# Attention and gated feed-forward on one core: another order of steps and copies for the first batch, output weights loaded in two parts

## The chip, the core and the metric

The kernel runs on one core of one Trainium2 chip. The metric is the device time of one execution in microseconds (us). Four runs of the kernel before the change took 518.34 to 519.17 us, with a median of 518.67 us. The profiled execution, which all rows come from, took 518.44 us; its span (first to last instruction) is 516.6 us.

The core has five engines with their own queues of instructions: TensorE (PE in the profile) multiplies matrices and writes into eight PSUM banks, ScalarE (ACT) and VectorE (DVE) copy and compute out of those banks, GpSimd (POOL) and SyncE (SP) issue the DMA transfers here. Each engine works through its queue in order.

## What is computed

```python
# q, k, v: (8 batches, 8 heads, 1024, 64);  E, F: (64, 1024)
k_proj = E @ k;  v_proj = F @ v                       # 64 projected keys and values per head
attn   = softmax(q @ k_proj.T / sqrt(64))
x      = (attn @ v_proj), heads side by side          # 8192 tokens x 512
gate   = sigmoid(x @ w_gate);  val = x @ w_val        # 512 -> 1536
out    = (gate * val) @ w_out                         # 1536 -> 512, float32
```

## The kernel before, in words

The work goes batch by batch; a batch is two blocks of 512 tokens. Attention for a batch gives `xT` (x with its 512 features on the partitions). The feed-forward part takes it block by block: `G` and `V` matmuls against `wG` and `wV`, a tanh on ACT in place of the sigmoid, a product on DVE into `hT`, and the output matmuls against `wO` (`oproj`, L1312). Later blocks build their products from seven half-size ones, with sums of weights and inputs made by DVE (`t_sums`, `vt_sums`, `xs_sums`, `product`).

The order in every queue is fixed when the kernel is built. `Plan.add` (L154) keeps one list of operations; each engine gets its own in that order, and a wait is set only where an operation reads or overwrites what another engine wrote. A PSUM bank counts as one object: every copy out of a bank waits for the copy before it if that was on another engine. From batch 1's second half on, a planner (`arranged`, L58) orders the list. Everything before that, which is all that the change edits, is an order written by hand: the sequence of calls at L1865 to L1905 for the first half of the first batch, and a list `todo` with additions by position (`put`, `on`) after it. The banks for the first half come from a written-out ring, `whole` (L358).

The first half of the first batch is worked out in two groups of four heads, R = 0 and R = 1:

- `start_loads` (L472) issues, on POOL's queue, k, q, k, q, v, v in halves by R (`load_kv_heads`, `load_q_half`), then the weights `wG` and `wV` in pieces. E and F come on SP's queue.
- `project_consts` (L604) turns E and F; `busy(n)` (L628) puts n filler matmuls of 128x512 into bank pF3 whose result nobody reads.
- `k_part(R)` (L1872) projects k (16 matmuls) and ACT copies the result to `kp` (`keep_k`, L660). `turn_k` (L684) transposes it and ACT copies to `kpD`. `qt(R)` (L715) transposes q into two banks, copied to `qT`.
- `sc(R)` (L738): scores, then two exponentials on ACT into `eT`. `den(R)` (L764): sums, and a reciprocal on DVE. `bc(R)` (L797): spreads the reciprocals over two banks; `keep(g)` (L818) copies bank g to `xu` on ACT.
- `v_part(R)` (L1877): projects v into two banks; `keep_v` (L670) makes four copies of a quarter each, on ACT, DVE, ACT, DVE, to `vpD`. `xo(R)` (L843): eight output matmuls into two banks, then DVE multiplies them with `xu` into `xT` (R = 0: two products of 128x512; R = 1: four of 128x256).
- `first_pair` (L1256) begins the feed-forward part: G for row groups 0 and 1 of `xT`, which R = 0 gives, then `xo(1)`, then V for the same row groups, then row groups 2 and 3.

`keep_v` has one more use, `v_alone` (L966), for batch 1 with all eight heads in one bank. `second_loads` (L1907) issues q, k and v of batch 1, four transposing DMAs of q on SP, and then one load of all `wO` on POOL's queue, which waits for the first two of these transposes. The loads of batch 2 come behind it in POOL's queue. The names `"wO"` and `"wO12"` in the lists of operands stand for `wO` and for the quarter of it that `t_sums(1)` overwrites.

Of the kernel before, what the change touches and what calls it, by code (L numbers as in the profile page):

```python
# [7 lines left out]
ALU = mybir.AluOpType  # L8
# [4 lines left out]
P = 128  # L13
# [224 lines left out]
def bass_linformer_attn__then__ffn_glu_sigmoid_kernel(  # L238
# [11 lines left out]
    B = q.shape[0]  # L250
# [6 lines left out]
    with contextlib.ExitStack() as es:  # L257
# [89 lines left out]
        class Ring:  # L347
# [9 lines left out]
        F0, F1, F2, F3 = FB  # L357
        whole = Ring(  # L358
            (A0, A1)
            + (A2, A3, F0, A0, A1, F1)  # L360
            + (A2, F2, A3, A0, F0)
            + (A2, A3, A1, F1, F2)
            + (A0, F0, A1, F1, A2, A3)
            + (A0, F3, A2, A3)
        )
        ffn, att = Ring(FB), Ring(AB)

# [289 lines left out]
                        tp=(0, 64 * h),  # L657
                    )

        def keep_k(bk, c0, R=None):  # L660
            width = 256 if R is None else 128
            act(
                kp[:, pairs(R), :],
                bank[bk][:, c0 : c0 + width],
                [],
                [("kp", x) for x in both(R)],
                b=bk,
            )

        def keep_v(bks, c0, engines, R=None):  # L670
            vv = vpD[:, :, :].rearrange("p (r h) d -> p r h d", h=2)
            width = 256 if R is None else 128
            for n, (h, g) in enumerate(((0, 0), (1, 1), (0, 1), (1, 0))):
                o = vv[64 * g : 64 * g + 64, pairs(R), h, :]
                i = bank[bks[h]][64 * h : 64 * h + 64, c0 : c0 + width].rearrange(
                    "p (r d) -> p r d", d=DH
                )
                ws = [("vpD", h, g, x) for x in both(R)]
                if engines[n] == "ACT":
                    act(o, i, [], ws, b=bks[h])  # L680
                else:
                    dve(lambda e, o=o, i=i: e.tensor_copy(o, i), [], ws, b=bks[h])  # L682

        def turn_k(ring, R=None):  # L684
            bk = ring.next()
            ob = bank[bk][:, :].bitcast(BF16)
            rs = range(NR)[pairs(R)]
            for n, r in enumerate(rs):
                for g in range(2):
                    mm(  # L690
                        bk,
                        ob[64 * g : 64 * g + 64, n * P : (n + 1) * P],
                        kp[:, r, :],
                        ident[:, :],
                        [("kp", r // 2), "ident"],
                        tr=True,
                        tp=(0, 64 * g),
                    )
            act(
                kpD[:, 2 * rs[0] : 2 * rs[-1] + 2, :].rearrange("p h c -> p (h c)"),  # L700
                ob[:, 0 : P * len(rs)],
                [],
                [("kpD", x) for x in both(R)],
                b=bk,
            )

        def VPD(R):
# [2 lines left out]
        def half_unit(hf, ring):  # L710
# [4 lines left out]
            def qt(R, engines):  # L715
                for rr, eng in enumerate(engines):
                    bk = ring.next()
                    ob = bank[bk][:, :].bitcast(BF16)
                    for x in range(2):
                        for t in range(2):  # L720
                            c = x * 2 + t
                            mm(
                                bk,
                                ob[:, c * P : (c + 1) * P],
                                Qb[:, 4 * R + 2 * rr + x, (2 * hf + t) * P : (2 * hf + t + 1) * P],
                                ident[:, :],
                                [("Q", hf, R), "ident"],
                                tr=True,
                            )
                    o = qv[:, R, 2 * rr : 2 * rr + 2, 256 * hf : 256 * hf + 256]  # L730
                    i = ob[:, 0:512].rearrange("p (x c) -> p x c", x=2)
                    ws = [("qT", hf, R, rr)]
                    if eng == "ACT":
                        act(o, i, [], ws, b=bk)
                    else:
                        dve(lambda e, o=o, i=i: e.tensor_copy(o, i), [], ws, b=bk)

            def sc(R):  # L738
                bks = [ring.next(), ring.next()]
# [57 lines left out]
            def bc(R):  # L797
                bks = [ring.next(), ring.next()]
                for c in range(4):
                    for g in range(2):  # L800
                        n = 2 * R + g
                        nn = slice(32 * n, 32 * n + 32)
                        mm(
                            bks[g],
                            bank[bks[g]][:, c * P : (c + 1) * P],
                            (bsel8 if hf else bsel8f)[nn, c, :, :].rearrange("p h d -> p (h d)"),
                            (rhl if hf else rden)[nn, 0:P],
                            ["bsel8", ("rhl", R)] if hf else ["bsel8f", ("rden", 0, R)],
                            tp=(32 * n, 0),
                        )  # L810
                def scales():
                    for g in range(2):
                        scale(R, g, bank[bks[g]], xu[:, 2 * R + g, :], [("xu", 2 * R + g)], bks[g])

                if hf:
                    return scales

                def keep(g):  # L818
                    act(
                        xu[:, 2 * R + g, :],  # L820
                        bank[bks[g]][:, :],
                        [],
                        [("xu", 2 * R + g)],
                        b=bks[g],
                    )

                return keep
# [15 lines left out]
            def xo(R):  # L843
# [14 lines left out]
                for g in range(2):  # L858
                    n = 2 * R + g
                    if hf:  # L860
                        act(xu[:, n, :], bank[bks[g]][:, :], [], [("xu", n)], b=bks[g])
                    elif R == 0:
                        scale(R, g, bank[bks[g]], xu[:, n, :], [("xu", n)], bks[g])
                if hf == 0 and R == 1:
                    for r in (2, 3):
                        for g in range(2):
                            cc = slice(256 * (r - 2), 256 * (r - 2) + 256)
                            dve(
                                lambda e, r=r, g=g, cc=cc: e.tensor_tensor(
                                    xT[s][:, r, hf, 256 * g : 256 * g + 256],  # L870
# [85 lines left out]
        def attention(b):  # L956
# [9 lines left out]
            def v_alone():  # L966
                bk = AA.take()
                turn_k(Ring((bk,)))
                AA.append(bk)
                bk = AA.take()  # L970
                project(1, 1, [bk, bk], 0)
                keep_v([bk, bk], 0, ["ACT", "DVE", "ACT", "DVE"])
                AA.append(bk)

            def sc_one(r, bks):
# [280 lines left out]
        def first_pair(blk, between):  # L1256
# [3 lines left out]
                for i in ii:  # L1260
                    mm_one(blk, m, i, n, pbs[m, n])

            step(0, "G", 0, 1)
            step(1, "G", 0, 1)
            if between:
                between()
            step(0, "V", 0, 1)
# [44 lines left out]
        def oproj(blk, tt, pb, cols=((0, DM),)):  # L1312
# [3 lines left out]
            for n, (c0, c1) in enumerate(cols):  # L1316
                if n:
                    pb = FF.take()
                for m in range(NF):
# [2 lines left out]
                        bank[pb][:, 0 : c1 - c0],  # L1322
                        hT[blk % 2][:, m, tt * P : (tt + 1) * P],
                        wO[:, m, c0:c1],
                        [("hT", blk % 2, m, tt // 2), "wO", "wO12"],
                        start=(m == 0),
                        stop=(m == NF - 1),
                    )
# [22 lines left out]
        def t_sums(n):  # L1351
# [1 line left out]
            B21, B22 = wO[:, H6:NF, 0:256], wO[:, H6:NF, 256:512]  # L1353
            T4, T3, T2 = [wT[:, i, :, :] for i in range(3)]
            o, a, b, op, r, w = {
                3: (T3, B22, B12, ALU.subtract, ["wO", "wO12"], [("wT", 3)]),
                2: (T2, T3, B11, ALU.add, ["wO", ("wT", 3)], [("wT", 2)]),
                4: (T4, B21, T2, ALU.subtract, ["wO", ("wT", 2)], [("wT", 4)]),
                1: (B12, B12, B11, ALU.subtract, ["wO"], ["wO12", ("wT", 1)]),
            }[n]  # L1360
            if n == 4:
                w = w + ["bsel8", ("kp", 0), ("kp", 1)]
# [28 lines left out]
        def product(blk, bk, A, B, start=False, stop=False, js=(0, 1), ms=(0, NF // 2), also=()):  # L1391
            h = hT[blk % 2]
            for j in js:
                for m in range(*ms):
# [8 lines left out]
                        rhs, k = wT[:, 4 - int(B[1]), m, :], ("wT", int(B[1]))  # L1403
                    else:
                        c = 256 * (B[2] == "2")
                        rhs, k = wO[:, m + H6 * (B[1] == "2"), c : c + 256], "wO"
                    mm(
                        bk,
                        bank[bk][:, 256 * j : 256 * j + 256],
# [456 lines left out]
        blocks_ready(0)  # L1866
        constants()
        project_consts()
        busy(5)
        qt, sc, den, bc, xo = half_unit(0, whole)  # L1870

        def k_part(R):  # L1872
            bk = whole.next()
            project(0, 0, [bk, bk], 0, R)
            keep_k(bk, 0, R)

        def v_part(R):  # L1877
            bks = [whole.next(), whole.next()]
            project(1, 1, bks, 0, R)
            keep_v(bks, 0, ["ACT", "DVE", "ACT", "DVE"], R)  # L1880

        k_part(0)
        qt(0, ("DVE", "DVE"))
        turn_k(whole, 0)
        busy(1)
        sc(0)
        busy(2)
        k_part(1)
        den(0)
        turn_k(whole, 1)  # L1890
        busy(1)
        qt(1, ("ACT", "DVE"))
        busy(1)
        sc(1)
        keep = bc(0)
        keep(0)
        keep(1)
        den(1)
        v_part(0)
        busy(1)  # L1900
        xo(0)
        keep = bc(1)
        keep(0)
        v_part(1)
        keep(1)  # L1905

        def second_loads():  # L1907
            load_q(1)
            load_k(1)
            load_v(1)  # L1910
            transpose_q()
            load(
                wO[:, :, :],
                moe_w_out.rearrange("(m p) c -> p m c", p=P),
                ["wO", "wO12"],
                "wO",
                r=turned()[:2],
            )


        todo, at = [], {}
# [200 lines left out]
```

## Time and profile before

| | |
|---|---|
| median of four runs | 518.67 us (518.34 to 519.17) |
| the profiled execution | 518.44 us, span 516.6 us |
| first FFN matmul to start | 21.19 us after the span's start |
| fillers in the first batch | 11 (5, 1, 2, 1, 1, 1) |
| landing of the k, q, k, q, v, v halves | 8.5, 9.8, 12.4, 13.7, 16.2, 18.8 us |
| load of `wO` | issued at 57.35 us, landed 12.2 us later; first matmul that reads it at 71.22 us |

Two rows of the page give the span in 40 slices of 12.9 us: the busy share of the DMA engines in tenths, and what they moved.

```profile
DMA  9999999899598778454946379374104330201013
GB/s 167 199 198 203 157 202 209 120 181 223 78 225 160 153 143 144 97 131 123 172 84 153 65 146 205 56 160 87 63 1 103 42 103 1 82 2 64 19 43 124
```

In a timeline row the first number is the start in us after the span's start, the second the time taken, then engine, line, operation, what is written <- what is read, shapes, and the count of merged instructions; in brackets the idle time of the engine before it and what ended it. Lines L385 (matmuls) and L389 (ACT) are helpers, so operations are told apart by their tiles: `KVs,EFT` is a projection, `gT,Qb` q being turned, `gT,wT` k being turned, `qT,kpD` scores, `eT,dsel` denominators, `gT,vT` the spread of reciprocals, `eT,vpD` outputs, and `gT` alone a filler. Some small tiles of the first batch lie inside buffers that later hold sums of weights, and the profile shows the buffer: `gT` is also `ident` and `rden`, `wT` also `kp`, `vT` also `bsel8f`.

### The profile page before, as it was taken

To read this page: it belongs to the slowest core of one execution; us is meant where nothing else is said; L and a number is where in the kernel's file an instruction comes from. 1 tells how busy PE (TensorE), PEld (TensorE's weight loads), DVE (VectorE), ACT (ScalarE), POOL (GpSimd) and SP (SyncE) were. 2 spreads that over 40 slices of the span, in tenths; PEclk is the share of its full clock that TensorE was granted. 3 is DMA by queue.
4 is the path that set the end of the run, shared out by engine and by line. 5 is a ranking of instruction groups with operands and counts; after the bars stand their busy time and mean duration, and the time that the engine had idled before them with its cause. 6 is when DMAs were issued, how large, how long until landed. Compare 5 with 4: busy or idle time off the path is not lost.

```text
span 516.6 us, 11359 instructions
## 1 busy us (share of the span) xinstructions
PE 505.0 (98%) x4595; PEld 410.4 (79%) x4595; DVE 409.9 (79%) x806; ACT 345.6 (67%) x646; POOL 40.4 (8%) x59
## 2 busy tenths in 40 slices
PE   5999999999999999999999999999999999999997
PEld 2545545888888888888888888888888888888885
DVE  4448789899779796987879888797968898787774
ACT  2555683867778677677767676777677766676752
POOL 9420201200200020000100020000000000000000
PEclk9999999999999999999999999999999999999999
DMA  9999999899598778454946379374104330201013
GB/s 167 199 198 203 157 202 209 120 181 223 78 225 160 153 143 144 97 131 123 172 84 153 65 146 205 56 160 87 63 1 103 42 103 1 82 2 64 19 43 124
DMA packets 105189, 63.13 MB, mean 122 GB/s; under 512 B 63024, under 2 KB 97328, under 8 KB 105136
## 3 DMA queue, kind: packets, MB, share of 16 engines
q0 software_dynamic: 33984, 29.89, 37.2%
q1 hardware_dynamic: 71152, 32.52, 27.4%
q8 instruction: 36, 0.59, 0.5%
q14 instruction: 17, 0.14, 0.1%
HBM read 60.29 MB, written 16.78 MB: 149 GB/s over the span
## 4 chain that ended last, share of the span: by engine, by line
PE 96%; DVE 1%; ACT 1%; DMA 1%; issue 0%; SPq 0%; DVEq 0%
PE pA L385 52%; PE pF L385 44%; DMA EF<-in_F_dram 1%; DVE hT L1830 0%; DVE vsnap L1708 0%; ACT vpD L389 0%; ACT vsnap L389 0%; DVE gT L780 0%; DVE vpD L682 0%; DVE ost L1435 0%; ACT sig L389 0%; DVE sig L1784 0%; ACT xu L389 0%; ACT qT L389 0%; ACT EF L389 0%
## 5 line engine op out<-in xcount | busy, mean ns | idle before, releaser
L389 ACT ACTIVATE sig<-pA 128x512 f32<-128x512 f32 x126 | 75.1, 596 | 45.9 <-PE pA L385 45.6
L1697 ACT ACTIVATE pF<-pA 128x512 f32<-128x512 f32 x99 | 58.5, 591 | 35.2 <-PE pA L385 30.1
L1708 DVE TENSOR_TENSOR vsnap<-pF,vsnap 128x512 f32<-128x512 f32 x90 | 61.7, 685 | 18.1 <-ACT vsnap L389 9.4
L1784 DVE TENSOR_TENSOR sig<-pF,sig 128x512 f32<-128x512 f32 x84 | 57.6, 685 | 4.4 <-PE pA L385 2.7
L385 PE MATMUL pF<-wO,hT 128*128 128x256 bf16 (+1 forms) x402 | 59.4, 285 | 0.0
L1830 DVE SCALAR_TENSOR_TENSOR hT<-sig,vsnap 128x512 bf16<-128x512 f32 x84 | 56.6, 684 | 1.0
L389 ACT ACTIVATE vsnap<-pA 128x512 f32<-128x512 f32 x84 | 50.2, 597 | 8.1 <-PE pA L385 7.8
L389 ACT ACTIVATE sig<-sig 128x512 f32<-128x512 f32 x84 | 52.7, 628 | 2.9 <-DVE sig L1784 2.5
L385 PE MATMUL pF<-xS,wV 128*128 128x256 bf16 x360 | 54.0, 273 | 0.1
L1830 DVE SCALAR_TENSOR_TENSOR hT<-sig,pF 128x512 bf16<-128x512 f32 x42 | 28.8, 685 | 30.7 <-PE pF L385 30.0
L385 PE MATMUL pA<-xT,gT 128*128 128x256 bf16 x336 | 50.5, 273 | 0.0
L385 PE MATMUL pA<-xT,vT 128*128 128x256 bf16 x336 | 50.4, 273 | 0.0
L385 PE MATMUL pF<-xS,wG 128*128 128x256 bf16 x336 | 50.4, 273 | 0.0
L385 PE MATMUL pF<-xT,wG 128*128 128x256 bf16 (+1 forms) x264 | 50.2, 311 | 0.0
L389 ACT ACTIVATE sig<-pF 128x512 f32<-128x512 f32 x66 | 39.5, 598 | 14.9 <-PE pF L385 12.5
L385 PE MATMUL pA<-wT,hT 128*128 128x256 bf16 x360 | 48.8, 273 | 0.5 <-ACT EF L389 0.4
L385 PEld LDWEIGHTS pF<-wO,hT 128*128 128x128 bf16 x402 | 38.7, 98 | 10.5 <-issue 0.8
L385 PE MATMUL pF<-xT,wV 128*128 128x256 bf16 (+1 forms) x240 | 41.5, 294 | 0.0
L385 PEld LDWEIGHTS pF<-xS,wV 128*128 128x128 bf16 x360 | 34.9, 98 | 6.1 <-DVE vsnap L1708 0.4
L385 PEld LDWEIGHTS pA<-wT,hT 128*128 128x128 bf16 x360 | 34.4, 98 | 6.0 <-ACT EF L389 1.4
L389 ACT ACTIVATE eT<-pA 128x512 bf16<-128x512 f32 x59 | 34.5, 594 | 5.4 <-PE pA L385 4.9
L385 PEld LDWEIGHTS pA<-xT,gT 128*128 128x128 bf16 x336 | 31.1, 98 | 7.5 <-issue 1.9
(158 smaller groups left out, 910.8 us busy)
## 6 DMA issues: line engine op xcount, KB each, us to landing
out_dram<-ost SPq DMA_DIRECT2D x61, 256.0 KB, 2.4
Qb<-in_q_dram POOLq DMA_DIRECT2D x7, 1024.0 KB, 10.8
KVs<-in_k_dram POOLq DMA_DIRECT2D x7, 1024.0 KB, 13.6
KVs<-in_v_dram POOLq DMA_DIRECT2D x7, 1024.0 KB, 17.8
wO<-in_moe_w_out_dram POOLq DMA_DIRECT2D x1, 1536.0 KB, 12.2
wG<-in_moe_w_gate_dram POOLq DMA_DIRECT2D x5, 256.0 KB, 17.1
wV<-in_moe_w_val_dram POOLq DMA_DIRECT2D x5, 256.0 KB, 17.7
KVs<-in_k_dram POOLq DMA_DIRECT2D x2, 512.0 KB, 8.2
```

The source lines that it names most:

```text
L385: return add("PE", lambda e: e.matmul(o, lhsT, rhs, **kw), r=r, x=[("bank", b)])
L389: return add("ACT", lambda e: e.activation(o, i, func, scale=scale), r=r, w=w, x=x, t=t)
L1697: lambda e: e.activation(bank[c][:, :], bank[a][:, :], AF.Copy, scale=1.0),
L1708: lambda e: e.tensor_tensor(o, bank[bk][:, :], o, ALU.add),
L1784: dve(lambda e: e.tensor_tensor(o, bank[bk][:, :], o, ALU.add), [key], [key], b=bk)
L1830: lambda e: e.scalar_tensor_tensor(o, sg.rearrange("p (j c) -> p j c", j=2), 1.0, x.rearrange("p (j c) -> p j c", j=2), ALU.add, ALU.mult,),
```

## The change

The written order of the first batch is another one, the ring of banks follows it, and copies go to other engines:

- Steps before: fillers 5, k0, q0, turn k0, filler, scores 0, fillers 2, k1, den 0, turn k1, filler, q1, filler, scores 1, bc 0, den 1, v0, filler, xo 0, bc 1, v1.
- Steps after: fillers 4, k0, fillers 2, q0, turn k0, filler, scores 0, filler, k1, fillers 2, turn k1, q1, den 0, fillers 2, scores 1, fillers 2, v0, den 1, bc 0, xo 0, bc 1, v1. That makes 14 fillers.
- Copies that go from ACT to DVE: k of group 1, both turned k, one of the two banks of bc 0. From DVE to ACT: one bank of q0 and the two DVE copies of v0. For q1 the two banks change engines. For v1 DVE makes the two copies of one bank and ACT those of the other, between ACT's two copies of bc 1, which change their order.
- `xo(0)` makes four products of 128x256, row group by row group, as `xo(1)` did; `xo(1)` now takes its second bank first. `first_pair` makes G row group by row group.
- `keep_v` takes the numbers of the copies and one engine. In `v_alone` ACT makes its two copies first, then DVE its two.
- `wO` is loaded in two halves by rows, each with its own name and semaphore (`wO0`, `wO1`), both behind the same wait; readers name the half that they read.

The core of the diff (banks of the ring, the helper `copied` that picks ACT or DVE, and the renamed operands left out):

```diff
-        def keep_v(bks, c0, engines, R=None):
+        def keep_v(bks, c0, ns, eng, R=None):
...
-            for n, (h, g) in enumerate(((0, 0), (1, 1), (0, 1), (1, 0))):
+            for n in ns:
+                h, g = ((0, 0), (1, 1), (0, 1), (1, 0))[n]
...
                     if hf:
                         act(xu[:, n, :], bank[bks[g]][:, :], [], [("xu", n)], b=bks[g])
-                    elif R == 0:
-                        scale(R, g, bank[bks[g]], xu[:, n, :], [("xu", n)], bks[g])
-                if hf == 0 and R == 1:
-                    for r in (2, 3):
-                        for g in range(2):
-                            cc = slice(256 * (r - 2), 256 * (r - 2) + 256)
+                if hf == 0:
+                    for r in (2 * R, 2 * R + 1):
+                        for g in (R, 1 - R):
+                            cc = slice(256 * (r - 2 * R), 256 * (r - 2 * R) + 256)
...
                 project(1, 1, [bk, bk], 0)
-                keep_v([bk, bk], 0, ["ACT", "DVE", "ACT", "DVE"])
+                keep_v([bk, bk], 0, (0, 2), "ACT")
+                keep_v([bk, bk], 0, (1, 3), "DVE")
...
-            step(0, "G", 0, 1)
-            step(1, "G", 0, 1)
+            step(0, "G", 0)
+            step(1, "G", 0)
+            step(0, "G", 1)
+            step(1, "G", 1)
...
-        busy(5)
+        busy(4)
...
-        k_part(0)
-        qt(0, ("DVE", "DVE"))
-        turn_k(whole, 0)
+        k_part(0, "ACT")
+        busy(2)
+        qt(0, ("DVE", "ACT"))
+        turn_k(whole, 0, "DVE")
         busy(1)
         sc(0)
+        busy(1)
+        k_part(1, "DVE")
         busy(2)
-        k_part(1)
+        turn_k(whole, 1, "DVE")
+        qt(1, ("DVE", "ACT"))
         den(0)
-        turn_k(whole, 1)
-        busy(1)
-        qt(1, ("ACT", "DVE"))
-        busy(1)
+        busy(2)
         sc(1)
+        busy(2)
+        v_part(0)(range(4), "ACT")
+        den(1)
         keep = bc(0)
-        keep(0)
-        keep(1)
-        den(1)
-        v_part(0)
-        busy(1)
+        keep(0, "ACT")
+        keep(1, "DVE")
         xo(0)
         keep = bc(1)
-        keep(0)
-        v_part(1)
-        keep(1)
+        keep(1, "ACT")
+        keep_1 = v_part(1)
+        keep_1((0, 2), "DVE")
+        keep_1((1, 3), "ACT")
+        keep(0, "ACT")
...
-            load(
-                wO[:, :, :],
-                moe_w_out.rearrange("(m p) c -> p m c", p=P),
-                ["wO", "wO12"],
-                "wO",
-                r=turned()[:2],
-            )
+            for x, w in enumerate((["wO0", "wO12"], ["wO1"])):
+                load(
+                    wO[:, H6 * x : H6 * x + H6, :],
+                    moe_w_out.rearrange("(m p) c -> p m c", p=P)[:, H6 * x : H6 * x + H6, :],
+                    w,
+                    f"wO{x}",
+                    r=turned()[:2],
+                )
```

## The prediction

> **What bounds it now.** I read the page first: busy shares, then the chain that ended last. TensorE is 98% busy, and the chain runs through matmuls almost all the way.
>
> ```profile
> PE 505.0 (98%) x4595; PEld 410.4 (79%) x4595; DVE 409.9 (79%) x806; ACT 345.6 (67%) x646; POOL 40.4 (8%) x59
> PE 96%; DVE 1%; ACT 1%; DMA 1%; issue 0%; SPq 0%; DVEq 0%
> ```
>
> So an edit pays only if it lets TensorE (PE) start its long run of feed-forward (FFN) matmuls earlier, or removes one of its few waits later. The PE timeline of the first 25 us shows the place. Columns: start, us taken, instruction, count, idle time before it and who ended it.
>
> ```profile
> 10.03 0.64 PE L385 MATMUL pA<-KVs,EFT 128*64 128x128 bf16 x16
> ...
> 15.51 0.41 PE L385 MATMUL pA<-qT,kpD 64*64 64x256 bf16 x8 [0.25 <-ACT qT L389]
> ...
> 18.07 0.39 PE L385 MATMUL pF<-gT 128*128 128x512 bf16 x1
> 19.19 0.30 PE L385 MATMUL pA<-eT,vpD 64*64 64x256 bf16 x2 [0.72 <-DVE vpD L682]
> ...
> 21.19 1.04 PE L385 MATMUL pF<-xT,wG 128*128 128x512 bf16 x4
> 22.18 0.84 PE L385 MATMUL pA<-eT,vpD 64*64 64x256 bf16 x8
> ```
>
> The reader is to see: the first FFN matmul starts at 21.19; before it PE stands 0.72 us for VectorE's (DVE's) copy of projected v. The chain of waits shows a second stop: the eight output matmuls that begin at 22.18 are cut in two, because their second bank is still being copied.
>
> ```profile
> 21.97 0.61 ACT xu L389
> 22.57 0.04 issue
> 22.62 0.41 PE pA L385 x6
> 23.02 0.97 PE pF L385 x4
> 23.99 0.03 issue
> 24.02 0.59 PE pF L385 x2
> ```
>
> From 24.02 PE hardly waits (the waits view has 0.9 us in three longer gaps up to the end). One of them, at 61.6, is touched by the change. The timeline of all engines there (pieces of other engines left out):
>
> ```profile
> 59.67 0.38 ACT L389 ACTIVATE vpD<-pA 64x256 bf16<-64x256 f32 x1 [0.16 <-PE pA L385]
> ...
> 60.08 0.43 DVE L682 CAST vpD<-pA 64x256 bf16<-64x256 f32 x1 [2.08 <-ACT vpD L389]
> ...
> 60.54 0.38 ACT L389 ACTIVATE vpD<-pA 64x256 bf16<-64x256 f32 x1 [0.49 <-DVE vpD L682]
> 60.94 0.60 ACT L389 ACTIVATE vsnap<-pF 128x512 f32<-128x512 f32 x1
> ...
> 61.60 0.61 PE L385 MATMUL pF<-xT,vT 128*128 128x256 bf16 x4 [0.15 <-ACT vsnap L389]
> ```
>
> Four copies of one bank alternate ACT, DVE, ACT, DVE, each waiting for the other engine. ACT's snapshot stands behind them, and PE behind the snapshot.
>
> **The first batch, walked through.** Step lengths on PE, start to next start, all from that timeline: half a projection 0.57 (10.03 to 10.60), q turns 0.55, k turns 0.235, scores 0.345, denominators 0.555, reciprocal spread (bc) 1.09 (15.85 to 16.94), outputs (xo) 0.34, a filler 0.23 (0.31 before a projection). Loads on POOL's queue are issued as before, so I keep their landings (issue plus time to landing): k halves 8.5 and 12.4, q 9.8 and 13.7, v 16.2 and 18.8.
>
> One filler less lets the first projection start at 9.6. Fillers are 0.43 apart until 9.47 and the projection at 10.03 already runs at twice that speed, so part of it is now at the slow pace: I let it end at 10.35 instead of 10.60. Two fillers (10.8), q turns (11.35) and k turns follow. The k copy onto DVE is not in the trace in this size (128x256 bf16): between 0.22 to 0.30 (64x128) and 0.42 (128x512); I take 0.29, halfway up by width. It follows the q copy on DVE: 11.73 to 12.02. PE sees a DVE result 0.05 to 0.15 later, so scores start at 12.1 (before: 11.97).
>
> Filler 12.45, second k projection 12.76; its copy, now on DVE (128x128 from PSUM; 0.30 by the same rows), ends 13.85. Two fillers cover that to 13.78; k turns 13.95, q turns 14.18, denominators 14.63, two fillers, scores 15.62. ACT's q copy (0.60) ends 15.43, so fillers and not data set this start. Up to here the change **loses 0.1** (15.62 against 15.51).
>
> From there PE has a straight run: scores 0.345, two fillers 0.54, first v half at 16.5 (landed 16.2), denominators 17.07, bc 17.64, xo 18.73, bc 19.07, second v half 20.16, first FFN matmul **20.73** against 21.19. What covers each step: ACT's four v copies (pitch 0.295, row of two in 0.56) run 17.25 to 18.4, ahead of xo at 18.73; DVE's reciprocal (0.96) ends 18.65, ahead of bc at 19.07; the bank kept by DVE (128x512 fp32, 0.69 as other DVE rows of that size) ends 19.54, then four half-width products (four in 1.42, pitch 0.335) give both halves of the first x row group at 20.3 and of the second at 21.0, needed at 20.73 and 21.16. The earliest weights land at 19.7. Two DVE products become four for 1.42 instead of 1.29, hidden as just shown.
>
> Second output: its v copies end at 21.55 on both engines, PE gets there at 20.73+0.99=21.72, so the stop at 22.57 goes. xo 21.72, V matmuls 22.06, which last 0.87; the products for the third x row group, from 22.25 on DVE with ACT's last bank at 22.12, end 23.0. So the matmul that stood at 24.02 starts at 23.1. **Gain 0.9** (0.74 if every DVE hand-off costs 0.15).
>
> From there PE is bound by its own work, so the gain passes on if no load is late. Second q halves landed at 29.5 and would be wanted at 30.5; k and v of batch 1 have 2 us and more; qT 3 us and more.
>
> **The two loads of the output weights.** One 1.5 MB load is issued at 57.35 and lands 12.2 later, 69.5; first use 71.22, now 70.0. The second issue costs POOL one more instruction of about 1.0, with the loads of batch 2 queued behind it; they stand in a queue that has been full since the start (the page's DMA row shows 9 tenths in most of the first ten slices), and are wanted a microsecond and more after landing (v at 81.4, used at 84.0). Value: nothing; its cover is the 0.5 us that even a single load would still have. Two 128 KB weight loads issued one after the other at 6.57 and 7.25 landed 0.4 us apart, so pieces cost little in a full queue.
>
> The Trainium skill, "DMA: Bandwidth & Descriptors", section "Anatomy of one DMA", speaks against splitting: each software-queued DMA carries about 2 us of fixed cost. By it the second half would land at 71.5, wanted at 71.4: 0.1 lost; by the 0.4 us row, nothing.
>
> **The copies at 60 us.** The same function now gives ACT its two copies, then DVE its two. Two ACT copies back to back end near 60.4, the snapshot starts when its matmuls are done (60.6) and ends 61.2, where PE would arrive by pace at 61.28 instead of 61.60. Gain 0.3 (0.2 at least, if the snapshot starts at 60.75). DVE's two copies end 61.2, before its next addition.
>
> **Sum.** 0.9 + 0.3 = 1.2. The profiled execution took 518.44 (span 516.6 and 1.8 around it), 0.23 under the median; 518.44 - 1.2 = 517.24, on the median's scale 517.5. Faster means by over 0.2%, 1.04 us, about what a measurement of this kernel can tell from no change.
>
> **Rivals.**
> 1. *The moved copies stand in the chain* (it does less than it says). k copy, turn, copy and scores are a chain, and three of the copies move to DVE. At 0.42 each and 0.15 per hand-off scores start at 12.3, second turns 0.37 later, second scores at 16.0: gain 0.5, in all 0.8: 517.8. For it: fillers already set 15.62, nothing is spare. Against it: DVE's row of 0.22 for half as much. The same time comes out if the 0.3 at 60 us is not had (517.8).
> 2. *More than reckoned*: the clock comes up earlier, or other waits also go (0.27 at 69.8, where the spacing of four matmuls is 0.71 instead of 0.44; 0.4 in the waits view, ended by ACT). About 517.0.
> 3. *Slower: the first v half.* It moves 1 us ahead in PE's order (17.50 to 16.5), and denominators, bc and xo stand behind it. It landed at 16.2; from 16.5 on each microsecond of lateness is one for all. At 17.7 the gain of 1.2 is gone, beyond that it is slower; a landing at 18.8, as the second half has, gives 519.8. Against it: no load ahead of it is touched, and the halves of k, q and v landed in order, 1.3 to 2.6 us apart.
>
> By the fillers' rows the clock came up between 9.5 and 10.0 (the page's granted clock shows 9 tenths or more in every slice, so the spacing has to be read); the one profile cannot show how it varies. The Trainium skill, "TensorE: Matmul & The Clock Gate", section "Part 1: The HAM clock gate", has a free-running window, so half a microsecond either way: both kernels would pay alike.
>
> **Chances.** Forecast (gain 0.9 to 1.5) 0.58; rival 1 0.24; rival 2 0.12; rival 3 0.06. Faster by over 0.2%: three quarters of the forecast and rival 2, 0.55; within: 0.41; slower 0.04. The range, 516.8 to 518.2, leaves out rival 3, the far ends of the two others: about 2 in 10.
>
> **What would show it.** Scores at 12.1 and 15.6, no wait before xo, first FFN matmul at 20.7, the 24.02 one at 23.1, no gap at 61.3; two wO loads, landing near 63.5 and 69.6, with no PE wait near 70. Wrong if PE waits before the first v projection, or for a DVE copy before either scores, or if the lead at 25 us is not there at 500.

## The result and the profile after

The changed kernel takes 517.61 us (median of 36 runs, 516.48 to 519.42), the kernel before 518.56 us (median of 55 runs, 517.17 to 519.96). The ratio is 0.9983, 95% interval 0.9978 to 0.9989: faster by 0.9 us, 0.17%, clear of noise but under the 0.2% named beforehand. The profiled execution's span went from 516.6 to 515.5 us.

The same two rows of the page, after:

```profile
PE 505.3 (98%) x4598; PEld 410.4 (80%) x4598; DVE 410.5 (80%) x809; ACT 345.3 (67%) x645; POOL 41.0 (8%) x60
PE 93%; DMA 3%; DVE 1%; POOL 1%; ACT 1%; issue 0%; SPq 0%; DVEq 0%; ACTq 0%; POOLq 0%
```

PE's work is the same and three fillers more. What is new is DMA with 3% in the chain; the page's row by lines gives 2% to the load of v and 1% to the stores of the output. The PE timeline of the first 25 us shows where loads are waited for:

```profile
12.92 0.64 PE L385 MATMUL pA<-KVs,EFT 128*64 128x128 bf16 x16 [0.29 <-DMA KVs<-in_k_dram]
...
16.06 0.60 PE L385 MATMUL pF<-gT 128*128 128x512 bf16 x2
16.84 0.64 PE L385 MATMUL pA<-KVs,EFT 128*64 128x128 bf16 x16 [0.17 <-DMA KVs<-in_v_dram]
...
20.84 1.04 PE L385 MATMUL pF<-xT,wG 128*128 128x512 bf16 x4
21.81 0.41 PE L385 MATMUL pA<-eT,vpD 64*64 64x256 bf16 x8
22.15 1.04 PE L385 MATMUL pF<-xT,wV 128*128 128x512 bf16 x4
23.35 0.38 PE L385 MATMUL pF<-xT,wG 128*128 128x512 bf16 x1 [0.16 <-DVE xT L868]
```

The wait of 0.72 for DVE's v copy is gone, and so is the cut in the eight output matmuls. PE now waits for loads: for the second k half and the first v half. The chain of waits, which before wound through copies on three engines, is short (start, us, what):

```profile
4.44 12.35 DMA KVs<-in_v_dram
16.80 0.04 issue
16.84 0.98 PE pA L385 x24
17.82 1.43 PE pF L385 x24
19.25 1.66 PE pA L385 x32
20.91 0.97 PE pF L385 x4
21.88 0.48 PE pA L385 x8
...
22.45 0.77 DVE xT L868 x2
23.21 0.14 issue
23.35 6.71 PE pF L385 x30
```

From the landing of the first v half to the first feed-forward matmul there is nothing but PE's own work, 4.04 us, and in this execution that landing sets the whole. The copies at 60 us, all engines:

```profile
58.99 0.78 ACT L389 ACTIVATE vpD<-pA 64x256 bf16<-64x256 f32 x2 [0.16 <-PE pA L385]
...
59.80 0.89 DVE L664 CAST vpD<-pA 64x256 bf16<-64x256 f32 x2 [2.48 <-ACT vpD L389]
59.94 0.60 ACT L389 ACTIVATE vsnap<-pF 128x512 f32<-128x512 f32 x1 [0.17 <-PE pF L385]
...
60.61 0.60 PE L385 MATMUL pF<-xT,vT 128*128 128x256 bf16 x4
```

The snapshot starts right behind ACT's two copies, as soon as its matmuls are done, and PE has no idle time in front of 60.61.

### The profile page after: what moved, and what is told of

The parts are those of the page before. It is cut to its first block, busy times and chain, and to the rows that moved or that the text cites. A ratio compares the mean times of both kernels' runs of the same rounds, so it can differ in the third digit from the quotient of the medians.

```text
span 515.5 us, 11367 instructions
## 1 busy us (share of the span) xinstructions
PE 505.3 (98%) x4598; PEld 410.4 (80%) x4598; DVE 410.5 (80%) x809; ACT 345.3 (67%) x645; POOL 41.0 (8%) x60
## 4 chain that ended last, share of the span: by engine, by line
PE 93%; DMA 3%; DVE 1%; POOL 1%; ACT 1%; issue 0%; SPq 0%; DVEq 0%; ACTq 0%; POOLq 0%
PE pA L385 50%; PE pF L385 43%; DMA KVs<-in_v_dram 2%; DMA out_dram<-ost 1%; DVE hT L1832 0%; POOL KVs L403 0%; DVE vsnap L1710 0%; POOL Qb L403 0%; ACT vsnap L389 0%; DVE xT L868 0%; DVE ost L1437 0%; ACT sig L389 0%; ACT pF L1699 0%; DVE sig L1786 0%; ACT EF L389 0%
## 6 DMA issues: line engine op xcount, KB each, us to landing
wG<-in_moe_w_gate_dram POOLq DMA_DIRECT2D x5, 256.0 KB, 17.7
```

## The experiments

The theory: two sources, the first batch (0.7 us in the profiles) and the copies at 60 us (0.3), with the first v landing as the new bound; the two loads worth nothing. The rivals: all of it is one source; the fillers delay work, or are needed; the two loads are needed. Order, banks and moved copies of the first batch stay together in all of them: what each is worth alone was not tried. "v" in this section is the first half of v of the first batch, "third-group matmul" the one that stood at 24.02.

### The parts alone: a_old_copies, b_new_copies, b_order_only

The changed kernel with the alternating copies back in `v_alone`:

```diff
-                keep_v([bk, bk], 0, (0, 2), "ACT")
-                keep_v([bk, bk], 0, (1, 3), "DVE")
+                for n, eng in enumerate(("ACT", "DVE", "ACT", "DVE")):
+                    keep_v([bk, bk], 0, (n,), eng)
```

> The changed kernel, with one part undone: in the single-bank projection of v for batch 1 the four copies alternate again, ACT, DVE, ACT, DVE. Theory (the gain of 0.9 to 1.1 us has two sources, about 0.7 in the first batch and 0.3 here): against the changed kernel 0.3 us is lost; the PE wait on ACT's snapshot near 60.6 us is back (0.3 between matmuls), the first feed-forward matmul stays near 20.8. Ratio to the kernel before about 0.9988. Rival (all of the gain comes from the first batch, and PE would wait for something else near 60 us anyway): no loss, ratio as the changed kernel, 0.9983.

The kernel before with only the new order of these copies:

```diff
-            for n, (h, g) in enumerate(((0, 0), (1, 1), (0, 1), (1, 0))):
+            for n, (h, g) in sorted(
+                enumerate(((0, 0), (1, 1), (0, 1), (1, 0))),
+                key=lambda x: x[0] % 2 if R is None else 0,
+            ):
```

> The kernel before, with only this part of the change: in the single-bank projection of v for batch 1 ACT makes its two copies, then DVE its two. Theory: 0.3 us gained, ratio about 0.9994, the gap between matmuls at 61.6 us closes (61.07 to 61.28 instead of 61.60) and the lead of 0.3 us is still there at 500 us. Rival: PE waits elsewhere for the snapshot or for DVE, nothing gained, ratio 1.0000.

The first batch's order alone: the changed kernel with the alternating copies of the first diff and the one load of `a_one_load` below.

> The kernel before with only the first batch's new order, banks and copies; the copies of batch 1 alternate as before and the output weights are one load. Theory: the first feed-forward matmul starts 4.0 us after the first v half lands (20.3 to 20.9), the matmul that stood at 24.02 starts at 23.1 to 23.4, ratio about 0.9987 (0.6 to 0.9 us gained). Rival (the two loads are needed once the rest is earlier): a PE wait of 0.3 us or more near 70 us, ratio 0.9993 or more.

| | ratio to before | v landed | first FFN matmul | third-group matmul | four matmuls `xT,vT` near 61 |
|---|---|---|---|---|---|
| before | 1 | 16.2 | 21.19 | 24.02 | 61.60, waited |
| b_new_copies | 0.9989 (0.9980 to 0.9997) | 17.0 | 21.54 | 24.37 | 61.63, no wait |
| b_order_only | 0.9985 (0.9976 to 0.9993) | 17.0 | 21.07 | 23.58 | 61.15, waited |
| a_old_copies | 0.9990 (0.9981 to 0.9998) | 17.0 | 21.35 | 23.86 | 61.55, waited |
| after | 0.9983 (0.9978 to 0.9989) | 16.8 | 20.84 | 23.35 | 60.61, no wait |

The times cannot divide the gain: the intervals are 0.9 us wide and overlap, and the two halves alone add up to more than the whole. The profiles say more. Where the copies alternate, 0.31 more lies between the matmuls there (61.07 to 61.60 before, 61.02 to 61.55 in a_old_copies); with the new order in the old kernel the wait is gone, and nothing takes its place: its waits view from 24 us on has two lines.

```profile
PE pA L385 <- DVE hS L1383: 0.3, 1, 0.3
PE pA L385 <- ACT EF L389: 0.2, 1, 0.2
```

For the first batch there is a pair with v landing at 17.0 in both: the old order reaches the third-group matmul at 24.37 (b_new_copies), the new one at 23.58 (b_order_only), 0.79 earlier, and 0.47 at the first FFN matmul. But the old order does not stand on that landing: it projects v at 17.86 there, and 0.35 of its time is lost to a clock that came up later than in the kernel before. The spacing of the matmuls shows it (the granted clock reads 1.00 in these stretches all the same). First k projection and q turns in b_new_copies:

```profile
9.43 1.06 PE L385 MATMUL pA<-KVs,EFT 128*64 128x128 bf16 x16
10.64 0.61 PE L385 MATMUL pA<-gT,Qb 128*128 128x128 bf16 x4
```

The first k projection in b_order_only:

```profile
9.25 0.64 PE L385 MATMUL pA<-KVs,EFT 128*64 128x128 bf16 x16 [0.16 <-DMA KVs<-in_k_dram]
```

From its first scores on, b_new_copies is 0.28 to 0.35 behind the kernel before (12.25 against 11.97, 21.54 against 21.19), although it had begun 0.6 earlier. a_old_copies, in the new order, also ran at half pace until about 11, and its second k projection stood at 13.16 all the same, as in b_order_only (13.18): there the k half, landed at 13.1, sets the start. So what the order is worth depends on the execution: 0.67 between the two profiles of the result, 0.79 in this pair, 0.44 to 1.02 over all pairings of before and b_new_copies with after and b_order_only. In eight of the nine profiles of the new order with the start loads as they were, PE begins to project v 0.04 after it landed; in the ninth (a_late_two) v landed at 16.12 and PE, after a late clock, came to it at 17.00.

a_old_copies shows a second bound: its second v half landed at 20.62 (19.3 in after, 19.55 in b_order_only), and its first FFN matmul came 0.73 behind that, at 21.35, later than the 21.04 that the first half asked for.

### The two loads: a_one_load, a_late_two, a_late_one

```diff
-            for x, w in enumerate((["wO0", "wO12"], ["wO1"])):
-                load(
-                    wO[:, H6 * x : H6 * x + H6, :],
...
+            load(
+                wO[:, :, :],
+                moe_w_out.rearrange("(m p) c -> p m c", p=P),
+                ["wO0", "wO12", "wO1"],
+                "wO",
+                r=turned()[:2],
+            )
```

> The changed kernel with the output weights in one load, issued as before. Theory (the load lands 0.3 to 0.9 us ahead of its first use, so the split is worth nothing in most executions): no PE wait near 70 us, ratio as the changed kernel, 0.9983 to 0.9986. Rival (landings vary by more than that from one execution to the next, so that one load costs): PE waits for it near 70 us in the profile, or the ratio is 0.9990 or more.

The other two hold the loads back until all four q transposes have landed (`r=turned()` in place of `r=turned()[:2]`), once with two loads and once with one.

> The changed kernel, with the two loads of the output weights held until all four q transposes have landed instead of two: issued about 1.2 us later, near 58.4. Theory: the halves land near 66 and 70.6, the first output matmul needs the first half at 70.2 and the seventh the second at 71.5: no PE wait, ratio as the changed kernel, 0.9983. Rival (a second load adds its own cost at the end of the transfer): second half after 71.5, PE waits for it.

> The same delay, with the output weights in one load. Theory: it lands near 70.6, the first output matmul at 70.2 waits for all of it, 0.3 to 0.6 us lost against the two loads, ratio about 0.9991. Rival (one load lands earlier than the second of two, since it has one issue less): lands before 70.2, no PE wait, no loss.

a_one_load came out at 0.9993 (0.9982 to 1.0004), and its profile shows the rival. The output matmuls, PE timeline:

```profile
70.72 0.74 PE L385 MATMUL pA<-eT,vpD 64*64 64x512 bf16 x8
71.89 1.46 PE L385 MATMUL pF<-wO,hT 128*128 128x512 bf16 x6 [0.43 <-DVE vsnap L1710]
```

The wait is put down to a DVE result, but the load was issued at 59.14 in this execution, 1.8 later than before, and landed at 71.75, 0.14 ahead of the matmul: PE waited for it. In b_order_only, also with one load, it landed at 70.12 for a first use at 70.77, without a wait. So one load is early enough in one execution and late in the next. The time doesn't settle what that is worth, since its interval reaches from 0.9982 to 1.0004. Nor is the load the main loss of the profiled execution: v landed at 17.58 there, so the third-group matmul stood at 24.38, 1.03 later than in the changed kernel, of 1.4 in the span. The twelve times fall into six from 516.9 to 517.6 and six from 518.6 to 519.1; the profiled one is among the longer.

With the delay the pair is clearer. One load: issued 60.15, landed 72.87, and PE stands 1.9 (again with DVE's name on it).

```profile
70.35 0.73 PE L385 MATMUL pA<-eT,vpD 64*64 64x512 bf16 x8
73.00 1.24 PE L385 MATMUL pF<-wO,hT 128*128 128x512 bf16 x5 [1.92 <-DVE hS L1382]
```

Two loads: landed 67.16 and 71.34, first uses 70.59 and 71.89, no wait. The expected sizes were wrong, not the mechanism: the ratios are 1.0017 (1.0003 to 1.0031) for one and 1.0000 (0.9991 to 1.0009) for two, where 0.9991 and 0.9983 were expected. In a_late_two later waits appear that the changed kernel has not, among them one for a transposed q of batch 2; the loads of batch 2 stand behind the held ones in POOL's queue.

```profile
PE pA L385 <- ACT sig L389: 0.4, 2, 0.2
PE pA L385 <- DMA qT<-Qb: 0.3, 1, 0.3
```

The Trainium skill, "DMA: Bandwidth & Descriptors", section "Anatomy of one DMA", gives each such transfer about 2 us of fixed cost. No run here shows that on the last landing: in the changed kernel the halves landed at 64.9 and 69.35, the single load before at 69.5.

### Fillers: a_no_fillers, a_fewer_fillers

```diff
         k_part(0, "ACT")
-        busy(2)
         qt(0, ("DVE", "ACT"))
         turn_k(whole, 0, "DVE")
-        busy(1)
         sc(0)
-        busy(1)
         k_part(1, "DVE")
-        busy(2)
...
         den(0)
-        busy(2)
         sc(1)
-        busy(2)
```

> The changed kernel without the ten fillers after the first k projection (the four ahead of it stay). Theory (they stand only where PE waits for a load or a copy anyway, and the first v half sets the rest): first feed-forward matmul within 0.1 us of the changed kernel's 4.0 us after the v landing, scores of the second group at most 0.15 earlier, same time, ratio 0.9983. First rival (some fillers delay work): 0.3 us or more gained, ratio 0.9977 or less. Second rival (they keep the matmuls at full pace): projections and scores of the first batch run at half pace, 0.5 us or more lost, ratio 0.9993 or more.

> The changed kernel with one filler instead of two in two places: after the second k projection and after the first denominators. Theory (they stand in waits, and the first v landing sets the rest): no gain, ratio 0.998 to 0.9986; second scores at most 0.15 us earlier, first feed-forward matmul 4.0 us after the v landing. Rival (in executions where v lands early the fillers set the start): 0.2 to 0.4 us gained, ratio 0.9976. Second rival (already two fillers fewer let the clock fall in some executions): single times above 520 us.

Without the ten fillers the ratio is 1.0016 (0.9999 to 1.0033), and the single times fall into two groups: seven from 517.8 to 519.2 and five from 521.0 to 521.7. The profiled execution is a long one (519.9 us of span), and its page shows why: the granted clock.

```profile
PEclk9599999999999999999999999999999999999999
```

By stretches of 3.4 us (columns: PE, PEld, DVE, ACT, POOL busy with counts, granted clock, DMA share, GB/s):

```profile
10.20:13.60 3.40, 2.00 (x36) 1.27 (x32) 0.72 (x2) 1.47 (x4) 3.40 (x5) 1.00 1.32 202
13.60:17.00 3.40, 2.85 (x44) 1.99 (x44) 1.05 (x4) 1.08 (x2) 3.40 (x6) 0.58 1.25 207
17.00:20.40 3.40, 3.23 (x44) 2.56 (x42) 1.87 (x2) 2.17 (x6) 2.24 (x3) 0.50 1.38 199
20.40:23.80 3.40, 3.40 (x34) 2.57 (x34) 2.05 (x5) 0.60 (x1) 0.00 (x0) 0.50 1.45 193
23.80:27.20 3.40, 3.40 (x29) 1.46 (x30) 0.57 (x2) 1.75 (x4) 0.00 (x0) 0.50 1.45 196
```

PE was busy for 2.0 of 3.4 us, waiting for copies and for a k half (0.84 at the longest), and then ran at half clock for some 13.7 us (the next stretch, 27.2 to 30.6, still shows 0.91): the spread of the reciprocals takes 2.08 instead of 1.16, and the first FFN matmul starts 7.2 after v landed instead of 4.0. The second rival holds: the fillers keep the clock. The mean granted clock on record for every execution says the same of the others: the five long ones had 0.986 to 0.990, the seven short ones 0.993 to 1.0. Five of the short ones lost some clock too (0.993 to 0.997) and were no longer for it (517.8 to 519.2) than the two at full clock (518.0 and 518.8). The first rival falls with it, since even the short executions are no faster than the changed kernel's.

a_fewer_fillers, with `busy(1)` in place of `busy(2)` behind the second k projection and the first denominators: 0.9982 (0.9971 to 0.9992), no time above 518.8, full clock, first FFN matmul 4.04 behind the landing. Two fillers fewer change nothing that can be measured.

### The v landing: a_late_v, b_late_v, a_late_v_fill

```diff
+            load_w(0, 0)
             for R in range(2):
                 load_kv_heads(1, v, R)
-            load_w(0, 0)
```

> The changed kernel, with the first two pieces of the feed-forward weights (two of 128 KB) issued ahead of the two v halves, so that these land about 1.2 us later (near 18.0 and 20.5). Theory (the first v half sets the start of everything behind it): the first feed-forward matmul follows the landing by 4.0 us, near 22.0, 1.2 later than in the changed kernel; ratio about 1.0005. Rival (PE's own steps set the start, as the prediction's walk had it, with 0.3 us of cover): 0.9 or less lost.

> The kernel before with the same two pieces issued ahead of the v halves. Theory (before, the first v half landed 1.3 us ahead of its projection at 17.5, so that much of a delay was covered): 0.0 to 0.6 lost, first feed-forward matmul near 21.2 to 21.8, ratio 1.0000 to 1.0012, so that the two orders come out nearly alike. Rival (v was as tight before): 1.2 lost, ratio 1.0023, and the new order keeps its 0.7.

| | ratio to before | v landed | first FFN matmul | behind the landing |
|---|---|---|---|---|
| a_late_v | 1.0034 (1.0006 to 1.0061) | 17.7 | 23.31 | 5.6 |
| b_late_v | 1.0012 (1.0002 to 1.0022) | 18.8 | 22.39 | 3.6 |

In both traces the record of the first of these four matmuls is missing, so the table has the start of its weight load (PEld), which elsewhere starts with the matmul. In a_late_v:

```profile
17.75 0.64 PE L385 MATMUL pA<-KVs,EFT 128*64 128x128 bf16 x16 [1.48 <-DMA KVs<-in_v_dram]
...
23.31 0.13 PEld L385 LDWEIGHTS pF<-xT,wG 128*128 128x128 bf16 x2 [0.17 <-issue]
23.71 1.49 PE L385 MATMUL pF<-xT,wG 128*128 128x512 bf16 x3 [0.33 <-issue]
```

With late v the old order loses 0.6 us and the new one 2.6 (1.0034 against 0.9983): the new order has given up the 1.3 us of cover that the old one had, the time by which v landed ahead of its use. Behind the landing the old order isn't longer: 3.6 us to the first FFN matmul, where the new one takes 4.04. But 2.6 is more than the lateness, 0.9 between the profiles of a_late_v and the changed kernel. In a_late_v PE stood 1.48 us for v, and the granted clock fell behind that stand:

```profile
13.60:17.00 3.40, 2.67 (x33) 1.20 (x32) 1.66 (x3) 1.68 (x3) 3.40 (x6) 1.00 1.28 205
17.00:20.40 3.40, 2.65 (x50) 1.95 (x50) 1.47 (x2) 1.64 (x5) 2.18 (x3) 0.90 1.31 202
20.40:23.80 3.40, 3.07 (x33) 2.73 (x35) 1.89 (x7) 0.96 (x4) 0.00 (x0) 0.50 1.45 196
23.80:27.20 3.40, 3.40 (x17) 1.00 (x17) 1.45 (x5) 0.82 (x2) 0.00 (x0) 0.60 1.45 196
```

So the same kernel was given more fillers for that stand:

```diff
-        busy(2)
+        busy(8)
         v_part(0)(range(4), "ACT")
```

> The kernel with the late v landing, and eight fillers instead of two ahead of the first v projection, so that PE does not stand while it waits for v (until 18.0). Theory (the extra loss with late v, 2.6 us instead of 1.2, is the clock, which fell to half after the 1.5 us stand in the profile): granted clock full throughout, first feed-forward matmul 4.0 us after the landing (or near 22.1 where v lands before 18.0), ratio near 1.0006, 1.2 us over the changed kernel. Rival (lateness itself costs more than one for one, for instance through the later loads): ratio stays near 1.003.

In its profile the clock is full in every slice, PE waits 0.25 for a v landing at 17.7, the same as in a_late_v, and the first FFN matmul starts at 21.73, 4.05 behind, where a_late_v had 23.31. The ratio is 1.0017 (0.9999 to 1.0034) against 1.0034, with intervals that overlap, but the clock on record for every execution divides the times:

| | granted clock 0.996 to 1.0 | granted clock 0.990 to 0.993 |
|---|---|---|
| a_late_v | four, 517.2 to 519.2 us | six, 520.3 to 524.4 us |
| a_late_v_fill | nine, 518.0 to 519.9 us | one, 523.4 us |
| b_late_v | ten, 517.4 to 519.8 us | none |

So the extra loss goes with the clock. With the clock held, the new order with late v takes as long as the old one with late v (1.0017 and 1.0012); that it gets slower than the old one by the lateness alone is not shown. Where v landed in the executions that were not profiled is not known.

### The stop before the second outputs: a_old_second

```diff
-        keep(1, "ACT")
+        keep(0, "ACT")
         keep_1 = v_part(1)
-        keep_1((0, 2), "DVE")
-        keep_1((1, 3), "ACT")
-        keep(0, "ACT")
+        for n, eng in enumerate(("ACT", "DVE", "ACT", "DVE")):
+            keep_1((n,), eng)
+        keep(1, "ACT")
```

> The changed kernel with the copies around the second output matmuls as they were: ACT's first bank of the second spread, then the four v copies on ACT, DVE, ACT, DVE, then ACT's second bank. Theory (the stop in front of the second output matmuls comes from this order): these start 0.5 to 0.8 us later than in the changed kernel (there 5.0 us after the first v landing) or are cut in two again, the first matmul of the third row group starts 0.4 to 0.8 later (there 6.55 us after the landing), ratio 0.9992 to 0.9998. Rival (DVE's products behind the second output matmuls set that matmul in any case): 0.2 us or less lost, ratio 0.9985.

0.9980 (0.9968 to 0.9991), and the stop does not come back. The PE timeline:

```profile
21.64 1.04 PE L385 MATMUL pF<-xT,wG 128*128 128x512 bf16 x4
22.61 0.41 PE L385 MATMUL pA<-eT,vpD 64*64 64x256 bf16 x8
22.95 1.04 PE L385 MATMUL pF<-xT,wV 128*128 128x512 bf16 x4
24.15 0.38 PE L385 MATMUL pF<-xT,wG 128*128 128x512 bf16 x1 [0.16 <-DVE xT L868]
```

The outputs start 0.97 behind the first FFN matmul and the third-group matmul 2.51 behind it, both as in the changed kernel. Yet ACT's last copy of the second spread ends at 22.93 here, after the outputs have begun. The difference to the kernel before is the ring: there the second outputs went into the two banks of that spread (A2, A3) and had to wait for its last copy; the new ring gives them the banks of the second v projection, and the spread has A1 and A0. So it was not the order of the copies that removed the stop, and what is left is the bank. That the new ring alone would do it in the old kernel was not tried.

## Why the prediction was right, and where it was off

- **What bounds the kernel, and that a lead at 25 us lasts**: right. The lead is 0.67 at the third-group matmul (24.02 to 23.35), 0.99 at the matmuls `xT,vT` (61.60 to 60.61), 1.09 in the span.
- **The walk**: scores were to start at 12.1 and 15.6 and did at 11.89 and 15.72; the k copy on DVE, taken at 0.29 between two rows, took 0.29. The first FFN matmul was put at 20.73 and stood at 20.84. Part of this is luck. The walk started from the first matmul of the old profile (6.02, when F had landed at 5.93); in the new one F landed at 5.40 and PE began at 5.49. That lead of 0.53 was then lost to a first k projection at half pace to its end (1.00 instead of 0.75) and to the second k half, which landed at 12.87 instead of 12.4.
- **The first batch's term** was 0.9 and measured 0.67 between the two profiles (0.44 to 1.02 with b_new_copies and b_order_only, by their landings and clocks). Two of its parts were too kind. The loads were kept at the landings of one execution, v at 16.2; in the profiled execution of the changed kernel it landed at 16.8, and PE waited. And DVE's two products before the third-group matmul ended 23.21, not 23.0, since DVE began them 0.64 and not 0.53 behind the outputs' start; PE followed 0.14 later.
- **The copies at 60 us**: 0.3 forecast, 0.31 measured, with the snapshot where it was put.
- **The sum**, 1.2, measured 0.9 by the times and 1.1 in the spans. 517.5 was forecast and 517.61 measured. "Faster by over 0.2%" was given the better chance (0.55); the gain of 0.17% stays just under it, for the 0.2 that the first term lacked.
- **The second stop** went, as forecast. The reason given, that v's copies are done before PE gets there (21.55 against 21.72), held (21.63 against 21.81) but leaves out the bank: with the old order of copies the stop stayed away too.
- **The two loads** were valued at nothing with a cover of 0.5. Mostly so, but the cover is not there in every execution: one load was waited for by 0.43 in a_one_load.
- **Rival 3** named the right mechanism: in the changed kernel the v landing is the bound. In the result PE waited 0.17 for it, a wait that the prediction had called a sign of being wrong; that the time came out even so rests on v having landed only 0.6 later than assumed. With v at 17.7 and the clock held (a_late_v_fill) the gain is gone, as rival 3 had it. Its price beyond that, one for one, left out the clock.
- **The clock**: the text said that both kernels would pay alike for its window. They did not: after a late clock the old order was 0.35 behind at the first FFN matmul (b_new_copies), while in the new one (a_old_copies) the wait for the second k half took it up. And the text saw the fillers only as work that delays or is hidden; they also keep the clock.

## What to carry to other kernels

Where an order is packed until a load is the bound, its cover is spent: read the landing times of several executions before you count the last half microsecond, since here the same load landed between 16.1 and 17.6. When a stop goes, check which resource it stood on; a bank shared by two steps looks like a slow copy. Dummy matmuls in a wait are not idle work if they keep TensorE's clock up, and a wait left bare can cost more than its own length.

## What the runs showed of the hardware

- **The granted clock halves after a stretch that is only partly idle.** a_no_fillers had PE busy for 2.0 of 3.4 us and no stand over 0.84 us, and lost half its clock for some 13.7 us; a_late_v stood 1.48 once and lost it for 6.8 us (0.7, 3.4 and 2.7 in the three stretches shown). b_late_v stood too (0.52 and 0.60), was busy 2.28 of 3.4 us in one stretch, and kept full clock. What tells these cases apart no run here shows. The Trainium skill, "TensorE: Matmul & The Clock Gate", section "Part 1: The HAM clock gate", lists the slow state as the default and as what follows at least one idle window of about 3.4 us. Here it came without any idle stretch of that length. Its remark that the window runs free of the kernel would fit that five executions of twelve were long and seven were not; no run here shows the window itself.
- **Landings differ between executions, all along the queue.** In the eleven profiles with untouched start loads the first k half landed between 8.4 and 9.8 us and the first v half between 16.1 and 17.6; the second v half between 18.8 and 21.2. That is more than the whole change is worth (0.9), and the times of one kernel spread by 3 us.
